# Top-k attention and a cosine-gated feed-forward: another order of issue within a slot, more buffers, weight decode in two steps

## The chip, the cores and the metric

The kernel runs on one core of one Trainium2 chip. The metric is the device time of one execution in microseconds. The engines are named as in the profile: PE (TensorE matmul; PEld is its weight load), DVE (VectorE), ACT (ScalarE), POOL (GpSimd) and SP (SyncE, which here only issues transfers).

## The reference

Two blocks follow each other. The first is attention in which each query keeps its 32 highest scores; the second is a feed-forward with the activation h * cos(h).

```python
# q, k, v: (8, 8, 576, 64) float32
scores = scale * np.matmul(q, k.transpose(0, 1, 3, 2))
kth = np.partition(scores, -top_k, axis=-1)[..., -top_k:-top_k + 1]   # top_k = 32
scores = np.where(scores >= kth, scores, -1000000000.0)
scores = scores - np.max(scores, axis=-1, keepdims=True)
attn = np.exp(scores)
attn = attn / (np.sum(attn, axis=-1, keepdims=True) + 1e-09)
attn_out = np.matmul(attn, v)
# (B, H, S, D) -> x: (4608, 512); w_in: (512, 2048); w_out: (2048, 512)
h = x @ w_in
g = h * np.cos(h)
out = (g @ w_out).astype(np.float32)
```

The two weight matrices arrive as 64-bit floats, and the kernel makes 32-bit floats of them itself.

## The kernel before

**Units and slots.** The 4608 rows of queries are cut into 36 tiles of 128 rows, and each tile into 4 pairs of heads. That makes 144 units, taken in turn. The main loop has one slot for each unit and two more. In slot i three units are at work: `u` (unit i) has its top-k made, `w` (unit i-1) its softmax, and `x` (unit i-2) its transposes and its product with v; the scores of unit i+2 are computed at the end of the slot.

- `scores` (line 177): matmuls into the PSUM tile `sc` (one buffer, line 178) and, directly behind them, one ACT copy of it to SBUF (line 192) as `s` (five buffers).
- `topk_round` (line 197): four rounds on DVE. Each finds 8 maxima for both heads (line 206), and the first three strike them out (line 209).
- `bounds` (line 213): on POOL, two small tiles `nb` and `nd` from the maxima. `softmax` (line 224): on ACT, a Prelu that pushes what lies under the bound far down (line 228), and the exponential with its sum (line 233). `add_eps` (POOL), `reciprocal` (DVE, line 246), `normalise` (POOL, line 251).
- `transpose_main` (line 256) and `transpose_tail` (line 267): PE transposes into PSUM (lines 264 and 272), ACT copies out (lines 265 and 273). `values` (line 275): matmuls with v (line 289) and an ACT copy into the transposed attention output `xT` (line 294).

**Feed-forward.** Rows are grouped into blocks: two of 128 rows, sixteen of 256, two of 128. `ff1` makes a part of h for a block (line 334), in PSUM tiles `mm` with two buffers. After two parts ACT evacuates half a chunk, scaled by 1/(2 pi), into a chunk `g` of 1024 columns (line 344). When a chunk is complete, its argument is reduced to one period on POOL into a tile `x` (lines 359 to 362). `sines` issues the sine on ACT (line 372), `gates` the product of chunk and sine on POOL (line 379), and `ff2` the matmuls with `w_out` (line 391), an ACT evacuation (line 397) and the store. In the two last slots and after them the reduction and the product go to DVE (lines 350 to 353). Chunks have `CHUNKS` = 5 buffers and the `x` tiles `XB` = 3.

**Feeding.** `feed(n)` issues up to n items of feed-forward (an `ff1` or an `ff2` call each) while there is credit: 4.2 are added in each slot, up to 6. It prefers `ff2` where the chunks have been gated and all weights are there, and else takes the next `ff1`, unless its block is not complete, its weights are not decoded, or a new chunk is needed and all chunk buffers are held. A block's chunks are released with its last `ff2`. What is left behind the slots is issued by a last loop, two items at a time.

**Weights.** 32 pieces of 128 x 512. `load_weights` fetches a piece of 512 KB on SP's queue into a buffer of the tag `x`; `decode_weights` takes it apart with three ACT operations (lines 114, 115 and 118), three on DVE (lines 119, 120 and 124) and two on POOL (lines 127 and 128). Its scratch has the tag `g`. Four pieces are decoded in a slot.

**Order.** The program is written in the order of the loop, but the compiler's scheduler may issue instructions in another order on each engine: the place in the program is a priority. Within an engine the issued order is fixed. Tiles of one tag share their buffers in turn.

Of the kernel before, what the change touches and what calls it, by code (L numbers as in the profile page):

```python
# [10 lines left out]
F32 = mybir.dt.float32  # L11
I32 = mybir.dt.int32
U32 = mybir.dt.uint32
AF = mybir.ActivationFunctionType
ALU = mybir.AluOpType

P = 128
# [13 lines left out]
def kernel(  # L31
# [9 lines left out]
    nc = tc.nc  # L41
# [46 lines left out]
        w_out.append(w)  # L88
        chunks.append((moe_w_out[f * P : (f + 1) * P, :], w))
    staged = {}  # L90
    CHUNKS, XB = 5, 3

    def load_weights(i):
        if i >= len(chunks):
            return
        src, dst = chunks[i]
        if not DECODE:
            nc.sync.dma_start(out=dst, in_=src)
            return
        st = ffw.tile([P, CW, 2], I32, tag="x", name="st", bufs=XB)  # L100
        nc.sync.dma_start(out=st.rearrange("p w i -> p (w i)"), in_=src)
        staged[i] = st

    def decode_weights(i):
        if not DECODE:
            return
        st = staged.pop(i)
        lo, hi = st[:, :, 0], st[:, :, 1]
        w = chunks[i][1]
        wi = w.bitcast(I32)  # L110

        both = ffw.tile([P, 2, CW], F32, tag="g", name="lo_sg", bufs=CHUNKS)
        r, sg = both[:, 0].bitcast(I32), both[:, 1]
        nc.scalar.mul(out=r, in_=lo.bitcast(U32), mul=2.0**-29)
        nc.scalar.sign(sg, hi)


        nc.scalar.activation(out=w, in_=hi.bitcast(F32), func=AF.Abs)
        nc.vector.tensor_scalar(out=w, in0=w, scalar1=2.0**-15, scalar2=None, op0=ALU.max)
        nc.vector.tensor_scalar(  # L120
            out=wi, in0=wi, scalar1=896 << 20, scalar2=3,
            op0=ALU.bitwise_xor, op1=ALU.logical_shift_left,
        )
        nc.vector.tensor_scalar(
            out=wi, in0=wi, scalar1=0x7FFFFFFF, scalar2=None, op0=ALU.bitwise_and
        )
        nc.gpsimd.tensor_tensor(out=wi, in0=wi, in1=r, op=ALU.add)
        nc.gpsimd.tensor_tensor(out=w, in0=w, in1=sg, op=ALU.mult)
# [46 lines left out]
            )  # L175

    def scores(u):
        sc = ps.tile([P, 2, 2, 512], F32, tag="sc", name="sc", bufs=1)
        for h in range(2):
            for j in range(2):  # L180
                d = slice(j * D, (j + 1) * D)
                for b, q0, rows, r0 in u["parts"]:
                    st = pairs[b, u["hp"]]
                    nc.tensor.matmul(  # L184
                        sc[r0 : r0 + rows, j, h, 0:HS],
                        st["q"][d, q0 : q0 + rows],
                        st["k"][d, h * HS : (h + 1) * HS],
                        start=True,
                        stop=True,
                    )  # L190
        s = u["s"] = work.tile([P, 2, S], F32, tag="s", name="s", bufs=5)
        nc.scalar.copy(  # L192
            out=s.rearrange("p j (h w) -> p (j h) w", h=2),
            in_=sc.rearrange("p j h w -> p (j h) w")[:, :, 0:HS],
        )

    def topk_round(u, rnd):
# [23 lines left out]
        nc.gpsimd.tensor_tensor(out=nd, in0=nb[:, :, 0], in1=nb[:, :, 1], op=ALU.subtract)  # L221
        u["nb"], u["nd"] = nb, nd

    def softmax(u):

        s, nb, nd = u["s"], u.pop("nb"), u.pop("nd")
        for j in range(2):
            nc.scalar.activation(  # L228
                out=s[:, j], in_=s[:, j], func=AF.Prelu, bias=nb[:, j, 1:2], scale=SCALE, alpha=FAR
            )  # L230
        den = u["den"] = small.tile([P, 2], F32, tag="den", name="den")
        for j in range(2):
            nc.scalar.activation(  # L233
                out=s[:, j], in_=s[:, j], func=AF.Exp, bias=nd[:, j : j + 1], scale=1.0,
                accum_out=den[:, j : j + 1],
            )
# [65 lines left out]
    for w in widths:  # L302
# [6 lines left out]
        t0 += w  # L309


    ff = {"live": 0, "now": 0, "weights": 0, "credit": 0.0, "end": False}
    first = deque((blk, i) for blk in blocks for i in range(2 * NF * blk["w"] // 512))
    second = deque(
        (blk, i, f) for blk in blocks for i in range(blk["w"] // P) for f in range(0, NF, 2)
    )
    waiting = deque()
    sined = deque()

    def ff1(blk, i):  # L320
# [23 lines left out]
        nc.scalar.mul(out=g[:, half * 512 : half * 512 + 512], in_=mm, mul=INV_2PI)  # L344
        if half == 0:
            return
        x = ffw.tile([P, 1024], F32, tag="x", name="x", bufs=XB)
        if ff["end"]:

            nc.vector.tensor_scalar(  # L350
# [2 lines left out]
            nc.vector.scalar_tensor_tensor(  # L353
                out=x, in0=x, scalar=MAGIC, in1=g, op0=ALU.subtract, op1=ALU.subtract
            )
            waiting.append((blk, g, x, ff["now"], -TWO_PI_BELOW))
            return
        gp = nc.gpsimd
        gp.tensor_scalar(out=x, in0=g, scalar1=1.0, scalar2=0.25, op0=ALU.mult, op1=ALU.add)  # L359
        gp.tensor_scalar(out=x, in0=x, scalar1=1.0, scalar2=MAGIC, op0=ALU.mult, op1=ALU.add)  # L360
        gp.tensor_scalar(out=x, in0=x, scalar1=-MAGIC, scalar2=1.0, op0=ALU.add, op1=ALU.mult)  # L361
        gp.tensor_tensor(out=x, in0=g, in1=x, op=ALU.subtract)  # L362
        waiting.append((blk, g, x, ff["now"], TWO_PI_BELOW))

    def sines(least):

        ready = [c for c in waiting if c[3] < ff["now"]]
        if not ready or (len(ready) < least and ready[0][3] + 4 > ff["now"]):
            return
        for blk, g, x, _, scale in ready:  # L370
            waiting.popleft()
            nc.scalar.activation(out=x, in_=x, func=AF.Sin, bias=halfpi, scale=scale)  # L372
            sined.append((blk, g, x))

    def gates():
        while sined:
            blk, g, x = sined.popleft()
            eng = nc.vector if ff["end"] else nc.gpsimd
            eng.tensor_tensor(out=g, in0=g, in1=x, op=ALU.mult)  # L379
# [41 lines left out]
            ff1(blk, i)  # L421
            n, ff["credit"] = n - 1, ff["credit"] - 1

    def decode(k):
        for _ in range(k):
            i = ff["weights"]
            if i < len(chunks):
                decode_weights(i)
                load_weights(i + 2)
                ff["weights"] += 1  # L430

# [11 lines left out]

    load_qk(0, 0)
    load_weights(0)
    load_qk(0, 1)
    load_weights(1)
    scores(units[0])  # L450
    for hp in range(2, NP):
        load_qk(0, hp)
    for hp in range(NP):
        load_v(0, hp)
    scores(units[1])
    for i in range(NU + 2):
        ff["end"] = i >= NU
        u = units[i] if i < NU else None
        w = units[i - 1] if 0 < i <= NU else None
        x = units[i - 2] if i > 1 else None  # L460
        for f, b, hp in at_slot.get(i, []):
            f(b, hp)
        ff["credit"] = min(ff["credit"] + 4.2, 6.0)
        ff["now"] += 1
        if w:
            bounds(w)
        if x:
            normalise(x)
        if u:
            topk_round(u, 0)  # L470
        decode(1)
        if w:
            softmax(w)
        gates()
        feed(2)
        if x:
            transpose_main(x)
        if u:
            topk_round(u, 1)
        decode(1)  # L480
        feed(1)
        if x:
            transpose_tail(x)
        feed(6)
        if w:
            add_eps(w)
        sines(2)
        if u:
            topk_round(u, 2)
        decode(1)  # L490
        if x:
            values(x)
        if i + 2 < NU:
            scores(units[i + 2])
        if u:
            topk_round(u, 3)
        if w:
            reciprocal(w)
        decode(1)
    while first or second:  # L500
        ff["now"] += 1
        ff["credit"] = 2.0
        gates()
        sines(1)
        feed(2)
        if ff["credit"] == 2.0:
            ff["now"] += 4


# [35 lines left out]
```

## Time and profile before

| what | us |
|---|---|
| median of three runs | 1837.81 |
| lowest and highest | 1831.09, 1840.10 |
| profiled execution, its own time | 1836.45 |
| its span, first to last instruction | 1834.70 |

The mean granted TensorE clock over the span is 0.970. The costliest groups of instructions, with their counts and the mean of one:

| line, engine | what | count | busy us | mean ns |
|---|---|---|---|---|
| 206 DVE | 8 maxima, of the rest | 864 | 611.1 | 747 |
| 334 PE | `ff1` matmuls | 2560 | 551.3 | 366 |
| 391 PE | `ff2` matmuls | 1152 | 539.7 | 606 |
| 209 DVE | strike out, from the rest | 576 | 423.4 | 743 |
| 233 ACT | exponential | 288 | 222.1 | 772 |
| 251 POOL | normalise | 288 | 215.6 | 749 |
| 228 ACT | mask | 288 | 212.0 | 773 |
| 192 ACT | copy of the scores | 144 | 160.7 | 1116 |
| 265 ACT | copy of the transposes | 288 | 154.3 | 582 |
| 372 ACT | sine, and its table loads | 72, 62 | 82.7, 79.5 | 1148, 1283 |

An instruction of a matmul that takes 32-bit operands leaves two records, so a count in the trace is twice the calls of the program there. A record's mean contains its overlap with its neighbours: in a dense run records follow each other in less than that. Busy time is a union in time for each engine, and where a stage has one engine near its full length, that engine or what feeds it sets the stage's end. The idle time of another engine then costs nothing.

### The profile page before, as it was taken

Reading aid. Unit: us, or ns where it says so; the run is one execution under the profiler, and the core shown is the slowest. Engines: PE = TensorE matmul, PEld = TensorE weight load, DVE = VectorE, ACT = ScalarE, POOL = GpSimd, SP = SyncE. Lnnn points to the kernel's source line nnn. Section 1 sums busy time; section 2 is a strip of 40 time slices with the busy share of each in tenths; the row PEclk is TensorE's granted clock in tenths of the full one; section 3 lists DMA queues with packets and bytes.
Section 4 is the critical chain, followed back from the end, with each engine's and each line's share of the span. In section 5 each row is a group of like instructions: output and inputs, shape, how many; then the busy total and the mean of one; then the engine's idle time right before and its main releaser. Section 6 shows DMA issues by size and latency. Waiting matters only on the chain.

```text
span 1834.7 us, 26443 instructions
## 1 busy us (share of the span) xinstructions
PE 1641.7 (89%) x9488; PEld 1077.8 (59%) x9488; DVE 1503.4 (82%) x3154; ACT 1173.5 (64%) x2056; POOL 854.2 (47%) x1103
## 2 busy tenths in 40 slices
PE   3477989989899989999999999999999999999897
PEld 2354566655656565565656575656666565656664
DVE  7999999979797878889797979899898979782211
ACT  5766768676667657576767676776767676762111
POOL 4786537362636535363636363554536363640000
PEclk9679989999999999999999999999999999999999
DMA  7430010001000110001000110011000100000000
GB/s 207 150 104 18 28 38 20 13 26 51 14 13 1 33 45 14 12 27 51 14 12 1 51 33 13 7 55 35 1 13 12 45 7 12 1 12 7 6 12 12
DMA packets 44228, 56.24 MB, mean 31 GB/s; under 512 B 10816, under 2 KB 27200, under 8 KB 44096
## 3 DMA queue, kind: packets, MB, share of 16 engines
q1 hardware_dynamic: 44096, 54.54, 9.6%
q8 instruction: 75, 1.23, 0.3%
q14 instruction: 57, 0.47, 0.1%
HBM read 45.09 MB, written 9.44 MB: 30 GB/s over the span
## 4 chain that ended last, share of the span: by engine, by line
DVE 52%; ACT 17%; POOL 15%; PE 12%; issue 3%; DMA 1%; SPq 0%; POOLq 0%; ACTq 0%
DVE m L206 27%; DVE rest L209 22%; PE o L391 6%; POOL x L362 5%; PE mm L334 4%; ACT s L228 4%; ACT s L233 3%; ACT x L372 3%; ACT s L192 2%; POOL x L359 2%; POOL x L361 2%; POOL x L360 2%; ACT L233 2%; ACT g L344 2%; PE o L289 1%
## 5 line engine op out<-in xcount | busy, mean ns | idle before, releaser
L206 DVE MAX8 m<-rest 128x8 f32<-128x576 f32 x864 | 611.1, 747 | 0.0
L334 PE MATMUL mm<-xT,w_in 128*128 128x256 f32 (+1 forms) x2560 | 551.3, 366 | 44.5 <-ACT g L344 40.3
L391 PE MATMUL o<-w_out,g 128*128 128x512 f32 x1152 | 539.7, 606 | 22.2 <-POOL g L379 11.5
L334 PEld LDWEIGHTS mm<-xT,w_in 128*128 128x128 f32 x2560 | 440.1, 193 | 142.8 <-ACT g L344 66.6
L209 DVE MATCH_REPLACE8 rest<-m,rest 128x576 f32<-128x576 f32 x576 | 423.4, 743 | 0.0
L391 PEld LDWEIGHTS o<-w_out,g 128*128 128x128 f32 x1152 | 207.8, 193 | 243.3 <-issue 217.3
L206 DVE MAX8 m<-s 128x8 f32<-128x576 f32 x288 | 203.4, 746 | 162.4 <-ACT s L192 162.4
L228 ACT ACTIVATE s<-s,nb 128x576 f32<-128x576 f32 x288 | 212.0, 773 | 145.4 <-POOL nb L216 145.4
L184 PE MATMUL sc<-k,q 64*128 64x288 f32 (+1 forms) x1280 | 239.6, 455 | 24.7 <-ACT s L192 15.3
L233 ACT ACTIVATE s<-s,nd 128x576 f32<-128x576 f32 x288 | 222.1, 772 | 2.1 <-POOL nd L221 1.3
L251 POOL TENSOR_SCALAR s<-s,rden 128x576 f32<-128x576 f32 x288 | 215.6, 749 | 1.3 <-DVE rden L246 0.7
L209 DVE MATCH_REPLACE8 rest<-m,s 128x576 f32<-128x576 f32 x288 | 211.7, 743 | 0.0
L216 POOL TENSOR_SCALAR nb<-m 128x4 f32<-128x4 f32 x144 | 29.6, 205 | 381.9 <-DVE rden L246 370.6
L264 PE MATMUL tp<-ident,s 128*128 128x128 f32 x1152 | 163.9, 282 | 40.0 <-POOL s L251 40.0
L264 PEld LDWEIGHTS tp<-ident,s 128*128 128x128 f32 x1152 | 136.2, 145 | 102.4 <-POOL s L251 54.8
L192 ACT COPY s<-sc 128x1152 f32<-128x1152 f32 x144 | 160.7, 1116 | 53.3 <-PE sc L184 52.2
L265 ACT COPY pT<-tp 128x512 f32<-128x512 f32 x288 | 154.3, 582 | 44.6 <-PE tp L264 44.6
L289 PEld LDWEIGHTS o<-pT,v 128*64 128x64 f32 x2560 | 134.9, 142 | 73.0 <-issue 36.9
L289 PE MATMUL o<-pT,v 128*64 128x128 f32 (+1 forms) x2560 | 171.7, 277 | 1.2 <-ACT pT L265 1.2
L184 PEld LDWEIGHTS sc<-k,q 64*128 64x128 f32 (+1 forms) x1280 | 115.1, 184 | 84.3 <-issue 37.3
L344 ACT ACTIVATE g<-mm 128x512 f32<-128x512 f32 x144 | 84.5, 587 | 125.2 <-PE mm L334 125.1
L379 POOL TENSOR_TENSOR g<-g,x 128x1024 f32<-128x1024 f32 x61 | 144.5, 2370 | 28.4 <-ACT x L372 25.1
(46 smaller groups left out, 1302.3 us busy)
## 6 DMA issues: line engine op xcount, KB each, us to landing
q<-in_q_dram SPq DMA_DIRECT2D x32, 288.0 KB, 3.0
out_dram<-ob SPq DMA_DIRECT2D x36, 256.0 KB, 2.0
st<-in_moe_w_in_dram SPq DMA_DIRECT2D x16, 512.0 KB, 5.2
v<-in_v_dram SPq DMA_DIRECT2D x32, 256.0 KB, 2.8
st<-in_moe_w_out_dram SPq DMA_DIRECT2D x16, 512.0 KB, 3.9
k<-in_k_dram SPq DMA_DIRECT2D x32, 144.0 KB, 3.3
k<-in_k_dram SPq DMA_DIRECT2D x32, 128.0 KB, 3.3
v_tail<-in_v_dram SPq DMA_DIRECT2D x64, 16.0 KB, 2.5
```

Source lines behind the costliest of these rows:

```text
L184: nc.tensor.matmul(sc[r0 : r0 + rows, j, h, 0:HS], st["q"][d, q0 : q0 + rows], st["k"][d, h * HS : (h + 1) * HS], start=True, stop=True,)
L192: nc.scalar.copy(out=s.rearrange("p j (h w) -> p (j h) w", h=2), in_=sc.rearrange("p j h w -> p (j h) w")[:, :, 0:HS],)
L206: nc.vector.max(m8[:, j, at], src[:, j])
L209: nc.vector.match_replace(rest[:, j], m8[:, j, at], src[:, j], NEG)
L228: nc.scalar.activation(out=s[:, j], in_=s[:, j], func=AF.Prelu, bias=nb[:, j, 1:2], scale=SCALE, alpha=FAR)
L233: nc.scalar.activation(out=s[:, j], in_=s[:, j], func=AF.Exp, bias=nd[:, j : j + 1], scale=1.0, accum_out=den[:, j : j + 1],)
L251: nc.gpsimd.tensor_scalar(out=s[:, j], in0=s[:, j], scalar1=rden[:, j : j + 1], scalar2=1.0, op0=ALU.mult, op1=ALU.mult,)
L264: nc.tensor.transpose(tp[:, c], s[:, j, k0 : k0 + P], ident)
L265: nc.scalar.copy(out=pT[:, :, j], in_=tp)
L289: nc.tensor.matmul(o[d, r], lhsT, rhs, start=c == 0, stop=c == NT)
L334: nc.tensor.matmul(mm[:, at : at + w], w_in[f // FC][:, c, (f % FC) * P : (f % FC + 1) * P], blk["xT"][:, c], start=c == 0, stop=c == NC - 1,)
L391: nc.tensor.matmul(o, g[:, at : at + P], w_out[f], start=f == 0, stop=f == NF - 1)
```

## The change

- **Buffers:** `CHUNKS` from 5 to 8, `XB` from 3 to 4.
- **Decode in two steps:** the three ACT operations of a piece are issued one step ahead of its DVE and POOL operations, in another order among themselves; a piece's load is issued at the start of the step two before. A slot has three steps instead of four, and one step stands ahead of the loop. A piece counts as decoded after its second step.
- **Order within a slot:** the scores' ACT copy is split off as `take_scores` and issued in the middle of the next slot; softmax is split into `mask` and `exponentials`, with an item of feed-forward and the main transposes between them; the chunk's reduction is split off `ff1` into two calls with their own places; one gate product is issued at the head of a slot instead of all that are ready; `reciprocal` stands ahead of the last top-k round, and `normalise` follows it in the same slot, a slot earlier than before. The three places of `feed` are 1, 2 and 6 items instead of 2, 1 and 6. Sines are issued at the end of a slot, for two chunks or when one has waited two slots (four before).
- **Start:** the first scores and their copy are issued ahead of the second weight load, and a decode step between the second unit's scores and their copy.

```diff
-    CHUNKS, XB = 5, 3
+    CHUNKS, XB = 8, 4
...
-    def decode_weights(i):
...
+    def decode_first(i):
+        st = staged[i][0]
         lo, hi = st[:, :, 0], st[:, :, 1]
         w = chunks[i][1]
...
-        nc.scalar.mul(out=r, in_=lo.bitcast(U32), mul=2.0**-29)
-        nc.scalar.sign(sg, hi)
-        nc.scalar.activation(out=w, in_=hi.bitcast(F32), func=AF.Abs)
+        nc.scalar.activation(out=w, in_=hi.bitcast(F32), func=AF.Abs)
+        nc.scalar.sign(sg, hi)
+        nc.scalar.mul(out=r, in_=lo.bitcast(U32), mul=2.0**-29)
+        staged[i] = [r, sg]
+
+    def decode_second(i):
+        r, sg = staged.pop(i)
...
+    def take_scores(u):
         s = u["s"] = work.tile([P, 2, S], F32, tag="s", name="s", bufs=5)
         nc.scalar.copy(
...
+    def reduce_first():
+        if not fresh:
+            return
+        blk, g = fresh[0]
         x = ffw.tile([P, 1024], F32, tag="x", name="x", bufs=XB)
+        fresh[0].append(x)
...
         gp = nc.gpsimd
         gp.tensor_scalar(out=x, in0=g, scalar1=1.0, scalar2=0.25, op0=ALU.mult, op1=ALU.add)
         gp.tensor_scalar(out=x, in0=x, scalar1=1.0, scalar2=MAGIC, op0=ALU.mult, op1=ALU.add)
         gp.tensor_scalar(out=x, in0=x, scalar1=-MAGIC, scalar2=1.0, op0=ALU.add, op1=ALU.mult)
-        gp.tensor_tensor(out=x, in0=g, in1=x, op=ALU.subtract)
-        waiting.append((blk, g, x, ff["now"], TWO_PI_BELOW))
+
+    def reduce_second():
+        if not fresh or len(fresh[0]) < 3:
+            return
+        blk, g, x = fresh.popleft()
+        if not ff["end"]:
+            nc.gpsimd.tensor_tensor(out=x, in0=g, in1=x, op=ALU.subtract)
+        waiting.append((blk, g, x, ff["now"], -TWO_PI_BELOW if ff["end"] else TWO_PI_BELOW))
...
-        ready = [c for c in waiting if c[3] < ff["now"]]
-        if not ready or (len(ready) < least and ready[0][3] + 4 > ff["now"]):
+        if not waiting or (len(waiting) < least and waiting[0][3] + 2 > ff["now"]):
             return
...
-    def gates():
-        while sined:
+    def gate(n):
+        for _ in range(min(n, len(sined))):
...
+    def decode():
+        i = ff["step"]
+        if i > len(chunks):
+            return
+        ff["step"] += 1
+        load_weights(i + 2)
+        if i < len(chunks) and DECODE:
+            decode_first(i)
+        if i > 0:
+            if DECODE:
+                decode_second(i - 1)
+            ff["weights"] = i
...
+    scores(units[0])
+    take_scores(units[0])
+    load_weights(1)
     load_qk(0, 1)
-    load_weights(1)
-    scores(units[0])
+    scores(units[1])
+    decode()
+    take_scores(units[1])
...
```

The body of a slot, after the change (`bounds(w)` stands ahead of it as before):

```python
        gate(1)
        reduce_first()
        if u: topk_round(u, 0)
        decode()
        if w: mask(w)
        feed(1)
        if x: transpose_main(x)
        if w: exponentials(w)
        if u: topk_round(u, 1)
        decode()
        feed(2)
        if x: transpose_tail(x)
        if 0 < i < NU - 1: take_scores(units[i + 1])
        if w: add_eps(w)
        if u: topk_round(u, 2)
        decode()
        reduce_second()
        if w:
            reciprocal(w)
            normalise(w)
        feed(6)
        if x: values(x)
        sines(2)
        if i + 2 < NU: scores(units[i + 2])
        if u: topk_round(u, 3)
```

The last loop issues up to two gate products, the reduction, the sines, again up to two gate products and two items of feed-forward in each turn.

## The prediction

> **What bounds it now.** I read the page, then the busy time of each engine in three stages, then the waits of one stage. The stages are cut by DVE, which runs the top-k of the 144 units one after another (a slot each): the start to slot 18, the loop of 126 slots from there, and the tail behind the last top-k.
>
> ```profile
> span 1834.7 us, 26443 instructions
> PE 1641.7 (89%) x9488; PEld 1077.8 (59%) x9488; DVE 1503.4 (82%) x3154; ACT 1173.5 (64%) x2056; POOL 854.2 (47%) x1103
> ...
> PE   3477989989899989999999999999999999999897
> ...
> DVE  7999999979797878889797979899898979782211
> ```
>
> DVE is full in the first slices and nearly idle in the last four, where PE still works at 9 tenths. The stages (busy us, instructions in brackets, of PE, PEld, DVE, ACT, POOL):
>
> ```profile
> 0.00:255.10 255.10, 170.09 (x1002) 110.29 (x1003) 239.90 (x474) 171.82 (x306) 154.58 (x181) 0.87 0.32 97
> 255.10:1645.20 1390.10, 1304.17 (x7751) 857.52 (x7750) 1228.73 (x2648) 964.37 (x1692) 696.33 (x917) 0.99 0.07 21
> 1645.20:1834.70 189.50, 167.46 (x738) 110.02 (x736) 34.76 (x34) 37.31 (x58) 3.27 (x7) 0.98 0.02 9
> ```
>
> The start is DVE's: 240 of 255 busy, the rest nearly all before the first top-k. The tail is PE's: 167 of 189. In the loop both are close: DVE needs 1228.7/126 = 9.75 us a slot, PE 1304.2/126 = 10.35, and a slot takes 11.03. PE idles 86 us there, DVE 161. One stretch shows why neither is full:
>
> ```profile
> 1032.50:1042.20 9.70, 9.70 (x59) 5.01 (x59) 9.70 (x23) 5.42 (x10) 1.99 (x5) 1.00 0.20 63
> ...
> 1051.90:1061.60 9.70, 8.45 (x65) 6.35 (x64) 9.70 (x23) 6.05 (x12) 1.99 (x5) 1.00 0.11 31
> 1061.60:1074.70 13.10, 11.06 (x88) 8.69 (x87) 9.74 (x22) 9.42 (x17) 10.83 (x14) 1.00 0.17 46
> ...
> 1087.00:1100.60 13.60, 13.37 (x92) 9.90 (x92) 9.81 (x21) 10.71 (x18) 10.39 (x11) 1.00 0.08 24
> ```
>
> These are single slots. Some last as long as DVE's work (9.70) with PE short of work; others hold so much feed-forward that PE takes 13 and DVE waits. The work is lumpy. What waits in the loop:
>
> ```profile
> DVE m L206 <- ACT s L192: 152.3, 52, 6.2
> ...
> PE tp L272 <- ACT pT L265: 44.9, 36, 3.5
> PE mm L334 <- ACT g L344: 34.1, 37, 2.9
> ```
>
> DVE's 152 us are waits for the next scores (they leave PE late), PE's 79 of 86 us are waits for two evacuations on ACT.
>
> **What one feed-forward item costs.** An item is one call of `ff1` or `ff2`. The chain of waits has dense runs in the tail:
>
> ```profile
> 1678.65 19.94 PE o L391 x46
> 1698.59 6.92 PE mm L334 x32
> ...
> 1764.96 3.58 PE mm L334 x32
> ```
>
> A 512-wide record costs 19.94/46 = 0.433 us; `ff2` makes 4: 1.73. A 256-wide one 6.92/32 = 0.216; `ff1` makes 8: 1.73. In 128-wide blocks 3.58/32 = 0.112 with 16 records: 1.79. I take 1.75 for all 576 items.
>
> **Part 1, eight chunk buffers.** A 256-row block takes 4 chunks and holds them until its last `ff2`. With 5 buffers, the next block may have one chunk at a time beside it. I followed `feed`, its credit and its counters slot by slot for both versions. Before: one block in 9 slots, though units for one come every 8; at the end of the slots 34 `ff1` and 46 `ff2` are left. The trace agrees: lines 334 and 391 have 1816 and 904 records in the loop, 227 + 226 items (followed: 230 + 226), and 184 of line 391 in the tail, which is 46. After: one block in 8 slots, 251 + 244 items in the loop, 13 + 28 left. So **39 items** leave the tail for the loop; slots with under two items fall from 18 to 10 of the last 86. The 32 items that the start can hold (two blocks) are the same.
>
> Tail before: 34 + 46 + 8 of the last two slots = 88 items x 1.75 = 154, two units of attention 8, idle 22, rest 5: 189.5. After: 49 x 1.75 = 86 + 8 + 22 + 5 = **121**.
>
> Loop: 39 x 1.75 = 68 more on PE: 1304 + 68 = 1372 busy. If the idle 86 stayed, 1458, and the whole change would give nothing. POOL gets 5 more chunks, each 3 x 1.05 + 2 x 2.37 = 7.9 us (lines 359 to 361; 362 and 379): 39 us against 694 idle.
>
> **Part 2, the order.** What it can take is the idle 86. Between the main transposes and the tail one (line 272), which waits for the copies of line 265, stood `feed(1)`; now `feed(2)`, 3.5 us, as long as the longest wait shown (3.5). And with fewer empty slots, there is something to feed. Line 334 waits when both PSUM buffers stand unread; more spread makes this rarer but the evacuation keeps its place on ACT. Bounds: 79 us gained at best, and at worst as much lost, since ACT's queue is reordered too. I take half gained, 40, because the stretch shows PE full (9.70 of 9.70) in slots with steady work: loop 1372 + 46 = **1418**, or 11.25 a slot.
>
> The moves inside a slot are costed at nothing: normalising a slot earlier (POOL, 2 x 0.75, same count; PE now waits only 3.1 us for it in the loop), the reciprocal ahead of the last top-k round (0.15 us; behind it on DVE stands that round, so a late denominator now stops DVE), one gate product at a time (POOL has room). Their cover is DVE's slack, 11.25 - 9.75 = 1.5 us a slot; if a wait exceeds it, each us costs 126. SP's order changes at the start: the second and third weight chunk go ahead of the q and k of later units. 512 KB at the 207 GB/s of the first slice is 2.5 us each; DVE needs unit 1 only at 23.0 and its copy now begins at 14.15, so 9 us cover that.
>
> **Part 3, decode.** Same 96 DVE, 96 ACT and 64 POOL operations. Three steps a slot instead of four end in slot 10, not 7. DVE's decode, 72 us (lines 119, 120 and 124), lies on DVE either way: 10.9 + 18 x 9.70 + 72 = 257.5 against 255.1. The feed-forward thus delayed has until slot 18. A fourth x buffer lets a chunk's load wait for a decode two steps back, no longer the last. The one gain is at the very start:
>
> ```profile
> 9.20 0.66 ACT L114 ACTIVATE lo_sg<-st 128x512 int32<-128x512 uint32 x1 [7.19 <-DMA st<-in_moe_w_in_dram]
> 9.76 1.11 ACT L192 COPY s<-sc 128x1152 f32<-128x1152 f32 x1
> ```
>
> The first copy of scores stands behind a decode that waits for its load; PE was done at 4.73 + 2.84 = 7.57. Now the copy comes first: 2 us. Start: **253**. Between 245 and 265, should the halves leave DVE waiting once or twice.
>
> **Sum.** 253 + 1418 + 121 = 1792 of span; 1836.45 - 1834.7 = 1.75 lies around it: 1794, 2.3% under the profiled run, whose time is 1.4 below the median 1837.8. So **1795**.
>
> Two rules stand beside these rows. The Trainium skill (Perfetto Trace Analysis, Identifying the Most-Contended Engine) says that matmul occupancy misjudges TensorE's headroom and that the share of weight loading is to be read instead. That share is 857.5/1390 = 62% in the loop, which would leave room for the 39 items at no cost: 253 + 1390 + 121 + 2 = 1766. The busy row says 94%; I follow it, since slots with full PE do grow past 9.70.
>
> The other speaks against the change: the skill's ScalarE: Activation LUTs, What ACT_TABLE_LOAD costs, wants functions grouped by table set and prices a switch at about 2.66 us with its drain, and the sines now wait two slots for company, not four. The rows show 57 table loads for 57 sines in the loop (line 372, 114 instructions), 1283 ns each: the scheduler already splits the pairs. At worst the 9 more sines in the loop make 18 more loads x 1.28 = 23 us of ACT against 426 idle. By the page's price they would be 48 us, still under it.
>
> **Rivals.** (a) All the waits go, chance 0.12: 253 + 1372 + 121 + 2 = 1748. For it: 79 of 86 us have two named causes that the change touches. Against: ACT does the same copies. (b) Nothing comes of it, 0.13: PE stays at 94% and the items cost in the loop what they cost in the tail, 1835; or the scheduler, for which the order is only a priority, issues much as now. For it: stretches of 200 us with quite different slots have PE busy 0.90 to 0.96 alike. (c) Slower, 0.30: the scores' copy. It was next to its matmuls and is now behind mask, evacuation, two pT copies, exponentials and tail copy: 2 x 0.77 + 0.59 + 2 x 0.58 + 2 x 0.96 + 0.26 = 5.5, a table load 1.28, itself 1.12: 7.9 of an 11.25 slot. ACT's waits in that stretch may take 3.3 us; from there on DVE starts late in every slot, its 1.5 us included. Half a us too much gives 1794 + 63 = 1857, one gives 1920. For it: 152 us of DVE's waits are for this very copy, and `sc` has one buffer. Against: it has a whole slot, and the scheduler may pull it forward.
>
> **Chances.** Forecast 0.45 (1765 to 1825), rivals 0.12, 0.13, 0.30. A measurement here tells about 0.5%. Faster 0.45 + 0.12 + 0.03 of (b) = 0.60, same 0.10, slower 0.30. The range 1750 to 1870 leaves out some 0.05 below and 0.13 above.
>
> **What would show it.** Line 391 in the tail: 112 records, not 184, and a tail near 121. Slots of 10.5 to 12 in place of 9.7 and 13.5. DVE's waits for line 192 about 190 us in the loop (126 x 1.5). PE's waits at lines 272 and 334 halved. First top-k near 8.8 us. Wrong if PE's idle in the loop stays at 86 or more, or DVE waits over 3 us a slot.

## The result, and the profile after

The changed kernel takes 1891.25 us (median of 4 runs, 1887.18 to 1895.81); the kernel before took 1838.95 us beside it (4 runs). The ratio is 1.029 (95% interval 1.025 to 1.034): **slower by 2.9%**. The forecast was 1795, its range 1750 to 1870, and the chance given to slower 0.30.

First the page of the changed kernel: span, busy time of each engine with its share of the span, and the busy tenths of PE and DVE in 40 slices.

```profile
span 1885.4 us, 26422 instructions
...
PE 1676.7 (89%) x9488; PEld 1087.9 (58%) x9488; DVE 1484.1 (79%) x3139; ACT 1170.8 (62%) x2060; POOL 896.3 (48%) x1128
...
PE   4569999898988898999898999899989898989997
...
DVE  7999989979796877788878778878787878787511
```

DVE is now nearly idle in the last two slices, not in the last four: the tail is shorter, as meant. In between, DVE's digits are mostly 7 and 8, where 7, 8 and 9 stood before. The three stages of the changed kernel (start to slot 18, loop of 126 slots, tail; busy us and instructions of PE, PEld, DVE, ACT, POOL; granted clock, DMA share, GB/s):

```profile
0.00:247.20 247.20, 177.29 (x997) 109.95 (x998) 232.09 (x474) 170.03 (x306) 156.91 (x183) 0.93 0.33 100
247.20:1768.90 1521.70, 1396.93 (x7983) 909.67 (x7982) 1233.01 (x2647) 976.22 (x1713) 737.09 (x941) 0.97 0.07 20
1768.90:1885.40 116.50, 102.50 (x511) 68.31 (x509) 19.03 (x19) 24.51 (x41) 2.33 (x6) 0.96 0.03 10
```

| us | before | named | after |
|---|---|---|---|
| start | 255.1 | 253 | 247.2 |
| loop | 1390.1 | 1418 | 1521.7 |
| of it PE busy | 1304 | 1372 | 1397 |
| of it PE idle | 86 | 46 | 125 |
| tail | 189.5 | 121 | 116.5 |

Start and tail gave even more than named. The loop took 104 us more than named: 79 of idle PE and 25 of busy PE. Three slots in a row show how (columns as above, one slot a line):

```profile
1222.50:1241.00 18.50, 18.20 (x92) 11.91 (x91) 9.81 (x22) 12.34 (x21) 13.50 (x17) 1.00 0.00 0
1241.00:1253.10 12.10, 9.59 (x47) 5.02 (x46) 9.79 (x21) 8.21 (x13) 6.17 (x7) 0.86 0.07 24
1253.10:1262.90 9.80, 9.80 (x49) 4.94 (x48) 9.77 (x22) 4.80 (x11) 1.30 (x3) 1.00 0.00 1
```

The first lasts 18.50 us with PE full in 18.20 of them and DVE at work in 9.81; in the second PE is idle for 2.5 us; the third is as long as DVE's own work. So the slots did not become steadier: of the loop's, 33 are longer than 13 us (20 before) and 17 are longer than 16 (none before). The feeding did. Counted in PE's order from the records of lines 187, 343 and 412, the feed-forward items between one unit's scores and the next have a standard deviation of 1.32 (1.65 before), and 6 of 124 such stretches have under two items (25 before).

The waits in the loop of the changed kernel (engine, tile and line that waits, what ended the wait; us in total, times, longest). Line 211 is the first maxima of a top-k (206 before), 197 the scores' copy (192), 254 the reciprocal (246), 233 the mask, 221 the bounds, 280 and 343 the tail transpose and `ff1` (272 and 334), 297 the product with v (289).

```profile
ACT s L233 <- POOL nb L221: 272.6, 97, 5.7
...
DVE m L211 <- ACT s L197: 207.0, 64, 9.4
...
DVE rden L254 <- POOL den L248: 81.6, 33, 8.0
...
PE tp L280 <- ACT pT L273: 47.4, 36, 3.9
PE mm L343 <- ACT g L353: 46.8, 27, 3.0
PE o L297 <- ACT pT_tail L281: 23.8, 19, 3.0
```

Two of these were hardly there in the loop of the kernel before:

```profile
DVE rden L246 <- POOL den L240: 8.7, 6, 3.5
...
PE o L289 <- ACT pT_tail L273: 0.4, 1, 0.4
```

DVE waits 207 us for the scores' copy (152 before) and 82 for the denominator (9 before). It is busy in the loop for 1233 us (1229 before), so nearly all that the loop grew by is idle time of DVE, 289 us against 161. PE's waits for ACT grew from 83 to 121 us, most of all at line 297. In 84 of the 207 us the scores lay ready in PSUM and the copy had not begun, since ACT had other work ahead of it; before it was 65 of 152. The 18.50 us slot shows such a wait (timeline of the changed kernel: start, us, engine, line; in brackets the idle time before it and what ended it):

```profile
1230.94 1.40 DVE L211 MAX8 m<-rest 128x8 f32<-128x576 f32 x2
...
1232.79 1.09 PE L297 MATMUL o<-pT,v 128*64 128x128 f32 x16
...
1233.14 2.35 POOL L400 TENSOR_TENSOR g<-g,x 128x1024 f32<-128x1024 f32 x1 [0.49 <-ACT pT_tail L281]
...
1234.03 1.24 PE L187 MATMUL sc<-k,q 64*128 64x288 f32 x8
...
1235.46 0.20 POOL L221 TENSOR_SCALAR nb<-m 128x4 f32<-128x4 f32 x1
1235.70 0.77 ACT L233 ACTIVATE s<-s,nb 128x576 f32<-128x576 f32 x1 [2.55 <-POOL nb L221]
...
1236.38 0.58 ACT L353 ACTIVATE g<-mm 128x512 f32<-128x512 f32 x1
...
1236.86 0.76 ACT L233 ACTIVATE s<-s,nb 128x576 f32<-128x576 f32 x1
...
1237.52 0.25 ACT L302 COPY xT<-o 128x128 f32<-128x128 f32 x1
1237.79 1.28 ACT L241 ACT_TABLE_LOAD   x1
...
1239.09 0.78 ACT L241 ACTIVATE s<-s,nd 128x576 f32<-128x576 f32 x1
...
1239.86 1.10 ACT L197 COPY s<-sc 128x1152 f32<-128x1152 f32 x1
...
1240.99 1.42 DVE L211 MAX8 m<-s 128x8 f32<-128x576 f32 x2 [8.65 <-ACT s L197]
```

The top-k before ends at 1232.34. The next scores leave PE only at 1234.03 + 1.24 = 1235.27, behind values and feed-forward. POOL runs a gate product of 2.35 us (line 400) just ahead of the bounds; ACT waits 2.55 us for the bounds, and behind them come two masks, an evacuation, a copy, a table load and an exponential, all ahead of the scores' copy at 1239.86. DVE has waited 8.65 us.

The two masks are those of the top-k that has just ended, and the program writes them behind this copy: a unit's `take_scores` stands in the slot before the one with the mask of the unit ahead of it. So here the scheduler has put the copy behind masks that need the whole top-k, and DVE can't go on until bounds, masks and copy are done. In ACT's issued order the copy stands behind one or both of these masks in 52 of the loop's 126 slots, and 230 of the 254 us between the end of one top-k and the start of the next lie there. Before, it was 28 slots, and 104 of 164 us.

### The profile page after: what moved, and what is told of

It reads as the page before. It is cut to its first block, busy times and chain, and to the rows that moved or that the text cites. A ratio compares the mean times of both kernels' runs of the same rounds, so it can differ in the third digit from the quotient of the medians.

```text
span 1885.4 us, 26422 instructions
## 1 busy us (share of the span) xinstructions
PE 1676.7 (89%) x9488; PEld 1087.9 (58%) x9488; DVE 1484.1 (79%) x3139; ACT 1170.8 (62%) x2060; POOL 896.3 (48%) x1128
## 4 chain that ended last, share of the span: by engine, by line
DVE 36%; POOL 24%; ACT 22%; PE 13%; issue 4%; DMA 0%; SPq 0%; POOLq 0%; ACTq 0%
DVE m L211 17%; DVE rest L214 16%; POOL s L259 6%; POOL x L384 6%; ACT s L233 5%; PE o L412 5%; ACT s L241 5%; PE mm L343 5%; POOL g L400 3%; POOL x L377 3%; ACT L241 3%; ACT x L393 2%; POOL x L375 2%; POOL x L376 2%; ACT s L197 2%
## 5 line engine op out<-in xcount | busy, mean ns | idle before, releaser
L343 PE MATMUL mm<-xT,w_in 128*128 128x256 f32 (+1 forms) x2560 | 580.3, 376 | 51.7 <-ACT g L353 48.7
L412 PE MATMUL o<-w_out,g 128*128 128x512 f32 x1152 | 557.0, 616 | 18.8 <-POOL w_out L131 10.6
L343 PEld LDWEIGHTS mm<-xT,w_in 128*128 128x128 f32 x2560 | 450.8, 197 | 163.7 <-ACT g L353 62.6
L259 POOL TENSOR_SCALAR s<-s,rden 128x576 f32<-128x576 f32 x288 | 215.6, 757 | 255.1 <-DVE rden L254 229.5
L187 PE MATMUL sc<-k,q 64*128 64x288 f32 (+1 forms) x1280 | 229.3, 458 | 19.0 <-ACT s L197 9.6
L248 POOL TENSOR_SCALAR den<-den 128x2 f32<-128x2 f32 x144 | 28.0, 194 | 423.9 <-ACT s L241 421.8
L297 PE MATMUL o<-pT,v 128*64 128x128 f32 (+1 forms) x2560 | 178.2, 276 | 11.7 <-ACT pT L273 11.7
L400 POOL TENSOR_TENSOR g<-g,x 128x1024 f32<-128x1024 f32 x66 | 156.1, 2365 | 62.2 <-ACT x L393 44.8
L384 POOL TENSOR_TENSOR x<-g,x 128x1024 f32<-128x1024 f32 x66 | 156.1, 2365 | 3.3
```

Source lines behind the costliest of these rows:

```text
L187: nc.tensor.matmul(sc[r0 : r0 + rows, j, h, 0:HS], st["q"][d, q0 : q0 + rows], st["k"][d, h * HS : (h + 1) * HS], start=True, stop=True,)
L259: nc.gpsimd.tensor_scalar(out=s[:, j], in0=s[:, j], scalar1=rden[:, j : j + 1], scalar2=1.0, op0=ALU.mult, op1=ALU.mult,)
L297: nc.tensor.matmul(o[d, r], lhsT, rhs, start=c == 0, stop=c == NT)
L343: nc.tensor.matmul(mm[:, at : at + w], w_in[f // FC][:, c, (f % FC) * P : (f % FC + 1) * P], blk["xT"][:, c], start=c == 0, stop=c == NC - 1,)
L384: nc.gpsimd.tensor_tensor(out=x, in0=g, in1=x, op=ALU.subtract)
L412: nc.tensor.matmul(o, g[:, at : at + P], w_out[f], start=f == 0, stop=f == NF - 1)
```

## The experiments

Each kernel was run in several rounds beside the kernel before; the ratio is to that, with its 95% interval. Where one is compared with the changed kernel or with another experiment, the medians are set side by side. "Held" means that the scheduler has to issue in the order of the program.

**Which part costs: buffers, order, reciprocal, copy.** The buffers alone, in the kernel before:

```diff
-    CHUNKS, XB = 5, 3
+    CHUNKS, XB = 8, 4
```

> The kernel before, with 8 chunk and 4 x buffers and nothing else. Followed through the feed, this moves the same 39 items from the tail into the loop as the whole change does. Theory A (the order within a slot is what costs): the tail falls from 189 to about 121 us and the loop grows from 1390 by 30 to 70, so 1795 to 1838. Theory B (39 more items in the loop make PE late in every slot, whatever the order): the loop grows by 130 as in the changed kernel, to about 1520, and the time is 1880 to 1900.

Measured: 1853.94 us, 1.009 (1.007 to 1.011). Loop and tail of it, columns as above:

```profile
255.40:1736.80 1481.40, 1372.91 (x7998) 905.63 (x7995) 1231.84 (x2649) 986.83 (x1719) 730.90 (x938) 0.98 0.07 21
1736.80:1852.30 115.50, 105.12 (x516) 68.41 (x514) 18.38 (x19) 26.42 (x43) 9.89 (x11) 0.96 0.03 10
```

The tail is 115.5 and PE is busy for 1372.9 us in the loop: both as predicted. But PE's idle time there also rose, 86 to 108, so the loop grew by 91 us, more than the 74 that the tail lost. The buffers, alone, lose 0.9%. ACT's issued order has changed with them: the copy stands behind the next masks in 53 slots (28 before).

The rest of the change alone, with the old buffers:

```diff
-    CHUNKS, XB = 8, 4
+    CHUNKS, XB = 5, 3
```

> The changed kernel with 5 chunk and 3 x buffers again. In the new order the feed issues nearly the same items in the loop with 5 buffers (492 against 495). Theory A (order): no difference to the changed kernel, 1880 to 1900. Theory B (buffers): back towards 1840.

Measured: 1880.26 us, 1.023 (1.022 to 1.025). Loop 1502.6, PE idle 119. So most of the loss comes with order and decode. The tail is 124.5 here and the loop holds 486 items (453 before, 489 with the buffers alone): the new order moves nearly the same items by itself. The items don't add, the losses nearly do: 17 and 43 us alone, 52 together.

Reciprocal and normalise behind the last round again, all else as changed:

```diff
         reduce_second()
-        if w:
-            reciprocal(w)
-            normalise(w)
         feed(6)
...
         if u: topk_round(u, 3)
+        if w:
+            reciprocal(w)
+            normalise(w)
```

> The changed kernel with reciprocal and normalise behind the last top-k round of the slot. The changed kernel shows 82 us of DVE waiting in the loop for the denominator at the reciprocal, with the last round queued behind it; before there were 9. If that wait is its own cost, it goes and the time falls by 60 to 82, to 1810 to 1830. If the scores' copy decides when DVE goes on, the wait only changes its name: line 197 waits grow from 207 to some 280 and the time stays at 1875 to 1895.

Measured: 1855.86 us, 1.011 (1.009 to 1.013): 35 us less than the changed kernel. The edit did reach DVE's issued order: the reciprocal, behind the sixth of a unit's eight maxima in 108 of 125 slots of the changed kernel, stands behind the eighth in 113. But DVE still waits 82 us at the reciprocal; what fell is its wait for the copy, 207 to 177. The move costs time, but not by the wait that was looked for.

The scores' copy directly behind its matmuls again:

```diff
-        if 0 < i < NU - 1: take_scores(units[i + 1])
...
         if i + 2 < NU: scores(units[i + 2])
+        if i + 2 < NU: take_scores(units[i + 2])
```

> The changed kernel with the scores' copy directly behind its matmuls again, as before. If the late place of the copy on ACT is the cost (207 us of DVE waits in the loop, 152 before, single ones up to 9.4 us against 6.2), those waits fall to about 150 and single ones to 6, and the time to 1820 to 1850. If the waits are due to the scores leaving PE late, nothing changes: 1880 to 1900.

Measured: 1908.38 us, 1.039 (1.037 to 1.040): slower still, and DVE's wait for the copy stays at 206 us. The copy's later place in the program is not the cause; in ACT's issued order it still stands behind the next masks in 57 slots.

**Is it the scheduler's rearranging?** Everything from the first load to the last loop issued as written, with 8 and 4 buffers and with 5 and 3, then PE alone, then ACT alone:

```diff
+    with tc.manual_schedule():
...
+    with tc.manual_schedule(engines={mybir.EngineType.PE}):
...
+    with tc.manual_schedule(engines={mybir.EngineType.Activation}):
```

> The changed kernel with every engine's instructions issued in the order in which the program is written, not rearranged by the scheduler. In the changed kernel the items of feed-forward per slot are as uneven in the trace (sd 1.54, up to 8 in a slot) as the followed feed is even (sd 1.30, at most 6), and 17 slots are over 16 us. Theory R (the rearranging is what costs: priorities do not give the written order): slots of 10.5 to 12, the loop 1390 to 1430, the time 1760 to 1810. Theory L (the order itself makes a chain of waits longer than 11 us in each slot): the same as the changed kernel or slower, 1880 and over.

Measured: 1991.06 us, 1.085 (1.083 to 1.088). Its waits in the loop:

```profile
DVE rden L254 <- POOL den L248: 323.2, 76, 12.3
...
PE o L412 <- POOL g L400: 137.5, 40, 6.0
```

The written order feeds PE about as evenly (a standard deviation of 1.39 items between scores) and is worse: DVE stands 323 us at the reciprocal, PE 138 us for gate products.

> The same with 5 chunk and 3 x buffers. The feed then issues 492 items in the loop against 495. If buffers matter only through the number of items fed, it is within 0.5% of the run with 8 and 4; if a held buffer stops a load or an evacuation, it is slower by 1% or more.

Measured: 1992.07 us, 1.087 (1.084 to 1.089), the same loss with the old buffers.

> The changed kernel with PE alone issued as written, the other engines rearranged. If the lumps of feed-forward on PE are the cost, this recovers most of what the fully written order gives: under 1830. If ACT's order (scores' copy behind mask and exponentials) is the cost, it stays at 1870 to 1900.

Measured: 1996.83 us, 1.089 (1.086 to 1.091). Its waits:

```profile
DVE m L211 <- ACT s L197: 304.4, 83, 14.1
...
PE mm L343 <- ACT g L353: 129.9, 59, 6.0
```

PE held alone gives the same loss by other waits: 130 us of PE for evacuations on ACT (47 in the changed kernel), and 304 us of DVE for the scores' copy.

> The changed kernel with ACT alone issued as written: 78 table loads in place of about 128, and the copies at their written places. If ACT's order is the cost: under 1830. If PE's lumps are: 1870 to 1900.

Measured: 1819.84 us, 0.992 (0.990 to 0.995): **71 us less than the changed kernel**, and less than before. Loop, and waits in it:

```profile
247.30:1703.20 1455.90, 1369.99 (x8016) 896.72 (x8014) 1235.94 (x2647) 915.58 (x1665) 738.98 (x941) 0.98 0.07 21
```

```profile
DVE rden L254 <- POOL den L248: 121.1, 47, 6.9
...
DVE m L211 <- ACT s L197: 97.0, 63, 6.8
...
PE o L412 <- POOL g L400: 51.9, 22, 6.0
```

PE's idle time is 86 us again, by other waits: 15 us for ACT (121 in the changed kernel) and 68 for POOL (3). The copy, which now does stand behind the mask, transposes and exponentials that the program writes ahead of it, starts 7.1 us after its scores are ready (2.0 in the changed kernel), since these are ready early. In no slot does it stand behind the masks of the top-k just made, and DVE waits 97 us for it, not 207.

**Is it ACT's order as such?** The kernel before with 8 and 4 buffers, ACT held:

```diff
-    CHUNKS, XB = 5, 3
+    CHUNKS, XB = 8, 4
...
+    with tc.manual_schedule(engines={mybir.EngineType.Activation}):
```

> The kernel before with 8 and 4 buffers and ACT issued as written, in its old order. If any fixed order on ACT helps, it is faster than the same buffers rearranged (1854): under 1830. If the new order within the slot is needed for it, it is 1850 or slower.

Measured: 1803.40 us, 0.982 (0.980 to 0.985): 50 us less than the same kernel with ACT rearranged (the buffers alone, 1853.94). So in both orders ACT as written takes time away, 50 and 71 us. The next two are the changed kernel with ACT held, the one with the reciprocal moved back as above, the other with 5 and 3 buffers:

> The changed kernel with ACT as written, and reciprocal and normalise behind the last top-k round. With ACT as written DVE still waits 122 us in the loop at the reciprocal with the last round behind it. If that round can run first, the waits fall under 40 and the time to 1770 to 1795; if the slot is bound by PE or by the softmax chain anyway, 1810 to 1830.

Measured: 1809.83 us, 0.986 (0.984 to 0.988). 10 us less than with ACT held alone; the wait at the reciprocal stays at 114. It is 46 us less than with the reciprocal moved back and ACT rearranged, where DVE issues the reciprocal at the same place in nearly all slots.

> The changed kernel with ACT as written and 5 chunk and 3 x buffers. If buffers matter only by the number of items that the feed can issue in the loop (492 against 495), the same as with 8 and 4: 1815 to 1830. If the three further chunks keep products and evacuations from waiting, slower by 1% or more.

Measured: 1844.91 us, 1.005 (1.003 to 1.006). Here the eight buffers are worth 25 us (with ACT rearranged they cost 11); PE waits 82 us for products with five chunks, 52 with eight.

**Which piece of ACT's order?** With ACT held it has 70 table loads, with the scheduler's order 128. So the sines of ACT held were split, one of each pair behind the exponentials:

```diff
+            if split["sine"]: sines(1)
...
+            split["sine"] = len(waiting) >= 2 or bool(waiting) and waiting[0][3] + 2 <= ff["now"]
             sines(2)
...
-        while waiting:
+        if waiting:
```

> The changed kernel with ACT issued as written, but of two sines that are due only one at the end of the slot, the other behind the exponentials of the next: 134 table loads instead of 70 (the changed kernel has 128), the rest of ACT's order the same. Theory T (the changed kernel's split pairs cost: 64 loads x 1.28 = 82 us of ACT): back to 1870 to 1900. Theory O (the order of copies, masks and exponentials): 1815 to 1845.

Measured: 1845.45 us, 1.005 (1.003 to 1.007), 134 table loads: 64 more, and 26 us more time. The split also makes half of the sines later, and PE's wait for products grows from 52 to 61 us; so a part of the 71 could be the loads. If so, the changed kernel with only exponentials and sines held in their written order (70 loads, the rest free) should win it back. In the first of these three kernels those are held, in the second the masks as well, in the third only copies and evacuations:

```diff
+        with tc.issue_after(last["act"].ins):
+            last["act"] = nc.scalar.activation(out=x, in_=x, func=AF.Sin, bias=halfpi, scale=scale)
```

> The changed kernel, rearranged as it is, but with sines and exponentials on ACT held in the order in which they are written relative to each other (an order on the queue, no wait): 70 table loads instead of 128. Copies, masks and evacuations stay free to move. If the split pairs are the cost of the rearranging, most of the 71 us between it and ACT as written (1891 against 1820) comes back: 1820 to 1845. By the single-sines run alone, which put 64 loads back for 25 us, some 25 come back: 1860 to 1870. If loads cost nothing here: 1885 and over.

> The same with the masks held in that written order too; copies and evacuations alone stay free. If masks that stand before a copy while they wait for the bounds are the rest of the cost, this comes to within 10 us of ACT as written: 1815 to 1830. If the copies' own places are, it stays where the run with pairs alone is.

> The changed kernel, rearranged, with the six kinds of copies and evacuations on ACT held in the order in which they are written relative to each other, and masks, exponentials and sines free (116 table loads). The opposite of the run with masks, exponentials and sines held (1949). If the places of the copies are what the rearranging costs: 1815 to 1850. If only one fixed order for all of ACT helps: 1880 and over.

Measured: 1914.45 us, 1.043 (1.041 to 1.044); 1949.37 us, 1.061 (1.060 to 1.063); 1921.53 us, 1.046 (1.043 to 1.048). All three are slower than the changed kernel, the last with 312 us of waits for the scores' copy. None of the three keeps the copy ahead of the next masks: it stands behind them in 70, 68 and 59 slots. A run that holds just this was not made, and no piece was found that does it by itself.

**A better version.** With ACT held, PE's waits are for gate products. In the kernel before with 8 and 4 buffers and ACT held:

```profile
DVE m L206 <- ACT s L192: 188.4, 81, 8.7
...
PE o L391 <- POOL g L379: 65.0, 34, 5.2
```

There `gates` stands ahead of the first `feed`, and a product made late in POOL's queue stops the `ff2` behind it. It was moved behind the last `feed`, so that a product is made in one slot for the `ff2` of the next:

```diff
-            gates()
             feed(2)
...
             feed(6)
+            gates()
```

> The kernel before with 8 and 4 buffers and ACT as written (1803), with the gate products issued behind the slot's last feed, not ahead of its first. PE waits 65 us in that kernel's loop for a product of the same slot. If those waits go and nothing takes their place: 1740 to 1770. If PE's lateness is DVE-paced or the waits move to other work: 1795 to 1810.

Measured: **1734.93 us, 0.945 (0.943 to 0.946)**, the fastest of all. Its loop, and the same two waits:

```profile
254.90:1621.40 1366.50, 1343.74 (x8043) 894.80 (x8038) 1231.77 (x2647) 915.50 (x1666) 747.04 (x944) 1.00 0.07 23
```

```profile
DVE m L206 <- ACT s L192: 126.4, 67, 7.2
...
PE o L391 <- POOL g L379: 3.6, 3, 2.0
```

PE's wait for products is gone (65.0 to 3.6), its idle time in the loop is 23 us, and the granted clock reads 1.00. The change's decode in two steps and its start, added to the kernel before with 8 and 4 buffers and ACT held:

> The kernel before with 8 and 4 buffers and ACT as written (1803), with the changed kernel's decode in two steps and its start. The changed kernel reached slot 18 at 247 us against 255. If that gain is the decode's own, slot 18 comes 6 to 8 us sooner and the time is 1793 to 1799; if it came from the order of the slot: 1800 to 1807.

Measured: 1801.46 us, 0.981 (0.980 to 0.983), against 1803.40 without: its start takes 253.7 us, against 253.2. This part gives nothing that can be told. Last, the new order, with ACT held, the reciprocal moved back, and the products moved as well:

```diff
-            gate(1)
             reduce_first()
...
             feed(6)
+            gate(2)
```

> The changed kernel with ACT as written, reciprocal and normalise behind the last top-k round (1810), and the gate products issued behind the slot's last feed. In that kernel's loop PE waits 53 us for products and DVE 114 at the reciprocal. If the products are the general cost, as in the old order (1803 to 1735): 1735 to 1765. If DVE's waits at the reciprocal, which the old order does not have, hold the slot up: 1790 to 1815.

Measured: 1760.18 us, 0.959 (0.958 to 0.961), 50 us less than without this move. Its waits on DVE:

```profile
DVE rden L254 <- POOL den L248: 116.3, 40, 7.7
...
DVE m L211 <- ACT s L197: 42.9, 41, 3.3
```

The copy hardly stops DVE now, but the denominator does, 116 us, against 8 in the fastest kernel. There the scheduler issues the reciprocal two to four maxima into the next top-k (in 122 of 125 slots), here directly behind the eighth, as written. With the same repairs the new order is 25 us behind the old one.

## Why the prediction was wrong, step by step

**Part 1, the tail: right.** Named 121, measured 116.5; line 412 (391 before) has the 112 records in it that were named. 38 items moved, not 39. PE's busy time with the buffers alone was 1372.9, named 1372. Two things were missed: the new order moves 33 of these items without the buffers (486 against 453), and a moved item costs more in the loop than PE's 1.75 us. With the buffers alone the idle time grew by 22 us too, and rival (b), "the items cost in the loop what they cost in the tail, 1835", was 19 us too low.

**Part 2, the order: here it failed.** The step is "I take half gained, 40, because the stretch shows PE full (9.70 of 9.70) in slots with steady work: loop 1372 + 46 = 1418". PE's idle time did not halve, it rose to 125, and busy PE came 25 us above the 1372, at a clock of 0.97 for 0.99 (see the last section). The step inferred that steadier feeding fills PE. The feeding became steadier (1.32 items for 1.65), but nearly all of PE's idle time is waits for ACT: 83 us before, 121 after, and 3 to 20 in the runs with ACT alone held. These waits depend on what ACT issues, and that is not what the program writes, which is what the step had priced. The written order is no cure in itself: followed on all engines it takes 1991 us. The same step had set the bounds as 79 us "gained at best, and at worst as much lost". The worse bound gives 253 + 1372 + 86 + 79 + 121 + 2 = 1913, and the measured 125 lies inside these bounds; but the range stopped at 1870, which leaves room for 36 of these 79. An unknown that was bounded from both sides was carried in full on the better side alone.

**The moves inside a slot, "costed at nothing".** The reciprocal's move cost 35 us as changed and 10 with ACT held, not nothing. Its cover, 1.5 us a slot, was an average: DVE's waits for the denominator come 33 times in 126 slots, up to 8.0 us long. But moving it back leaves those waits as they were; how the 35 us arise isn't shown.

**Rival (c)**, priced at 1857 to 1920, holds the measured time, and its chain is in the trace above. As a cause it was only half right: the copy does come too late on ACT, but behind masks that the scheduler, not the program, put ahead of it. With the copy moved back the kernel is slower still; with ACT held, where it stands exactly as far back as feared, DVE waits for it 43 to 136 us in the runs of the new order, and 177 to 312 us in all those where ACT was rearranged.

**What cost the time** is shown as far as this: ACT issued as written brings the changed kernel from 1891 to 1820 and the kernel with the buffers alone from 1854 to 1803; in the changed kernel's order the reciprocal's place costs 35 us with ACT rearranged and 10 with ACT held. The traces point at the copy behind the next masks: 28 such slots before, 43 to 70 in the other kernels with ACT rearranged, none with ACT as written. That this alone does it is **not shown**: every piece held by itself made things worse, none of them was this pair, and holding ACT also changes what the scheduler does on the other engines (the reciprocal's place on DVE, above), which was not fully separated. Small edits around the changed kernel (old buffers, one move undone, some instructions held) gave 1856 to 1949 us, 2 to 3% either way, as much as the whole change; how much of that is an edit's own effect and how much the scheduler's answer is open.

**Part 3, the start: right in size, not in reason.** Named 253, measured 247.2, and the gain wasn't the first top-k: that begins at 10.7, not near 8.8, with three decode instructions ahead of it on DVE. It began at 8.8 once ACT was held. The 8 us are DVE's decode, whose 96 instructions take 63.9 us in place of 72.0 (see the last section), and DVE's idle time ahead of slot 18 is the same, 15. In the old order with ACT held the two-step decode gained nothing.

**The other signs.** "Slots of 10.5 to 12": no. "DVE's waits for line 192 about 190": 207. "Waits at lines 272 and 334 halved": 45 to 47 and 34 to 47. "Wrong if PE's idle in the loop stays at 86 or more": it did.

**The two rules.** The loop grew by 91 us with the buffers alone while PE's weight loads were busy in 905.63 of 1481.40 us, 61%. The Trainium skill (Perfetto Trace Analysis, Identifying the Most-Contended Engine) would have read that share as headroom; here the busy row was the better guide, and still too hopeful.

Table loads: the run with 64 more of them, 1283 ns each or 82 us in all, was 26 us longer, and a part of that may be the later sines. The Trainium skill (ScalarE: Activation LUTs, What ACT_TABLE_LOAD costs) prices a switch at about 2.66 us with its drain; by that price the 64 would be an estimated 170 us of ACT's time. The rows of this run show no drain: a load starts 18 ns (median) behind the instruction before it, and the next one follows 12 ns behind the load.

## What to carry to other kernels

Where a scheduler may rearrange, compare the issued order with the written one before pricing an edit of the order, and try each engine held as written: one held engine was worth more here than the whole change, and another held cost over 5%. Put the product that an engine will wait for a whole stage ahead of its user, not just ahead of it in the program (68 and 50 us here). And if a term is bounded from both sides, let the range carry both.

## What was not expected of the hardware

**DVE beside POOL.** The same decode instruction takes 0.41 us, or up to 2.51. Timeline of the kernel before:

```profile
14.69 0.41 DVE L120 TENSOR_SCALAR w_in<-w_in 128x512 int32<-128x512 int32 x1
...
17.60 1.41 POOL L128 TENSOR_TENSOR w_in<-w_in,lo_sg 128x512 f32<-128x512 f32 x1
17.80 0.75 DVE L206 MAX8 m<-rest 128x8 f32<-128x576 f32 x1
...
18.47 0.82 DVE L120 TENSOR_SCALAR w_in<-w_in 128x512 int32<-128x512 int32 x1
...
128.50 2.54 POOL L379 TENSOR_TENSOR g<-g,x 128x1024 f32<-128x1024 f32 x1
...
128.82 2.51 DVE L119 TENSOR_SCALAR w_out<-w_out 128x512 f32<-128x512 f32 x1
```

The instruction of line 120 takes 0.41 us at 14.69, where POOL is idle, and 0.82 at 18.47, while POOL's product of two tensors runs (17.60 to 19.01). The one of line 119 at 128.82 takes 2.51, beside a longer product. Both end 0.28 to 0.29 us after POOL's instruction does, and so do all 57 of the 96 that take over 0.5 us: they stand until POOL is done, rather than run slower. The MAX8 at 17.80, within the first of these products, takes its usual 0.75. So where these decode instructions fall beside POOL's work changes DVE's sum: 72.0 us before, 63.9 in the changed kernel, 53.5 with all engines held. The Trainium skill (GPSIMD Engine Reference, Specifications) has GpSimd's SBUF interfaces shared with VectorE, with contention where DVE runs in a two-port mode or reads two SBUF tensors; the rows agree in that one kind of DVE instruction is stopped and another is not; in which mode the decode instructions run, no row shows.

**PE's busy time depends on its idle time.** Stretches of 20 us in the loop of the changed kernel (the granted clock is the third number from the end):

```profile
1160.00:1180.00 20.00, 19.66 (x128) 11.58 (x129) 17.00 (x38) 9.63 (x19) 3.85 (x9) 1.00 0.09 29
1180.00:1200.00 20.00, 15.16 (x102) 11.50 (x100) 15.49 (x35) 10.82 (x22) 9.63 (x13) 1.00 0.00 1
1200.00:1220.00 20.00, 19.66 (x116) 14.70 (x118) 19.34 (x41) 16.68 (x28) 12.06 (x13) 0.91 0.00 1
```

A stretch with 4.8 us of idle PE is followed by one at a clock of 0.91. Cut into 300 stretches of 5 us, the loop shows it throughout: behind a stretch with at most 0.3 us of idle PE the mean clock is 1.00 (209 of them), behind one with over 2 us it is 0.81 (22 of them). Over the loop, nearly the same matmul records took 1344 us at a clock of 1.00 in the fastest kernel, 1373 at 0.98 with the buffers alone, 1397 at 0.97 in the changed one and 1407 at 0.94 with all engines held. Time and clock multiplied give 1322 to 1355 in all four. So the runs with more idle PE pay for it again in slower matmuls, and a price for an item that is read from a dense run holds only while PE stays dense.
